# The channel part of a Fourier block: jobs in a written order across steps, no GpSimd, and a plain first step for the second batch

## The chip, the cores and the metric

The kernel runs on one core of a Trainium2 chip. The metric is device time in microseconds of one execution; the kernel before takes 647.47 us (median of three runs, 646.49 to 647.83). The engines are named as in the trace: PE is TensorE's matmul, PEld its weight load, DVE is VectorE, ACT is ScalarE, POOL is GpSimd, SP is SyncE, whose queue issues most DMAs.

## The reference

Two batches of 768 tokens go through three blocks: bucketed attention, a gated convolution block and a Fourier block. The change lies in the last one:

```
X = fft(fft(x, axis=1), axis=2)
u = x + real(X)
un = (u - mean(u)) / sqrt(var(u) + 1e-6)
ch = max(un @ w_ch1, 0) @ w_ch2        # w_ch1: 512 x 2048, w_ch2: 2048 x 512
out = u + ch
```

The last two lines with the normalisation are called the channel part here. The weights come as float64.

## The kernel before, in words

Matmuls run on float32 values split in two parts, a high part of few mantissa bits and a low part that holds the rest, so that each product is three matmuls: high by high, high by low and low by high. Any operand of a matmul therefore needs an ACT copy that rounds to the high part and a DVE subtraction that gives the low part.

*Mixing.* The function `mixing` computes the Fourier transform of both batches. Its loop has 14 turns. From turn 8 on it also prepares batch 0 for the channel part: `stats` (mean and variance on DVE, then a square root on ACT), `scale` (reciprocal and shift on DVE, then two ACT activations that write the normalised `un`), `u_transpose` on PE and `u_parts` (high part `bh` on ACT, low part `bl` on DVE). Tiles of tokens are treated in pairs `kt` and `kt + 3`, so there are three such pairs per batch. Behind the loop the last transform of batch 1 is added up (`both`), and POOL writes `u[1]`.

*Channel part.* The hidden width of 2048 is cut in 16 blocks `f` of 128. A block's first layer (`first`) is 12 matmuls per half of the tokens (128 by 384), its relu is taken as high part on ACT and low part on DVE (`relu_high`, `relu_low`), and its second layer (`second(m, t)`) is three matmuls (128 by 512) for each of six token tiles `t`, which add up in six PSUM banks `acc`. When the batch changes, the six sums are added into `u` on DVE.

Batch 0 does blocks 0 to 3 in this plain way (`PLAIN`). Everything else goes in 14 steps of one batch and two blocks each, where the four products of a 2 by 2 block matrix are made with seven products of half size (a Strassen scheme; `product`, six matmuls each). It needs sums of weights (`weight_steps`, four jobs: two sums, four combinations, high part, low part) and sums of tokens (`token_steps`, the same four; for batch 1 `turned`, which also transposes). Seven products share two PSUM tiles `x` and `y`; their interim results are copied to `snap` by ACT (lines 1651, 1662, 1665), added to by DVE (1654, 1671, 1674), and then go through the relu.

Weights are loaded as float64 chunks of 512 KB (`channel_load`) and turned into high and low part by integer arithmetic, six jobs a chunk (`channel_steps`, lines 148 to 171: six DVE instructions, two on ACT). A step converts two chunks.

Each engine runs its instructions in the order in which the program issues them. That order is set by hand: a step calls its products one after the other, and between them `after(c)` runs the background jobs (conversion of weights, weight sums, token sums) that a small table has put at place `c`, always those of the same step. Some of the sums run on POOL (`eng=nc.gpsimd`): the low parts of batch 1's token sums, the weight sums for blocks 0 to 3 and 6, 7, and two thirds of batch 0's token sums.

Of the kernel before, what the change touches and what calls it, by code (L numbers as in the profile page):

```python
# [37 lines left out]
PLAIN = 4  # L38

# [67 lines left out]
def block_kernel(  # L107
# [24 lines left out]
    def from64(words_of, raw, dst, half=False, parts=P, spare=False):  # L132
# [7 lines left out]
        a, e, g = (words_of(n, x)[:parts] for x in "aeg")  # L140
# [6 lines left out]
        def s0():  # L147
            nc.vector.tensor_scalar(a, hi, 0x7FFFFE00, None, op0=ALU.bitwise_and)

        def s1():  # L150
            nc.scalar.activation(a, a, AF.Relu, scale=8.0, bias=col[:parts, b : b + 1])

        def s2():
            nc.vector.tensor_scalar(g, hi, 0x1FF, 15, op0=ALU.bitwise_and, op1=ALU.logical_shift_left)
            nc.vector.scalar_tensor_tensor(g, lo, 17, g, op0=ALU.logical_shift_right, op1=ALU.bitwise_or)

        def s3():
            nc.vector.scalar_tensor_tensor(a, hi, -(2 ** 31), a, op0=ALU.bitwise_and, op1=ALU.bitwise_or)  # L158
            nc.vector.tensor_scalar(e, a, -(2 ** 23), None, op0=ALU.bitwise_and)

        def s4():
            if spare:
# [7 lines left out]
        def s5():  # L170
            nc.scalar.copy(dst()[0], fold(a.bitcast(F32)))  # L171
# [834 lines left out]
    def channel_steps(k, spare=False):  # L1006
# [5 lines left out]
        st = from64(channel_words, wraw[k], lambda: w, spare=spare)  # L1012
        third = st[3]

        def last_words():
            third()
            channel_load(k + 2)

        st[3] = last_words
        return st  # L1020

    def stats(b, kt):

        for t in (kt, kt + 3):
            st = wst[0].tile([P, 6], F32, tag="st", name="st")
            nc.vector.bn_stats(st, u[b][:, t, :])
            nc.vector.bn_aggr(mu[b][:, t, :], st)
        ks = slice(kt, kt + 4, 3)
        nc.scalar.activation(rstd[0][:, b, ks], mu[b][:, ks, 1], AF.Sqrt, bias=col[:, 6:7])

    def scale(b, kt):
# [3 lines left out]
        nc.vector.scalar_tensor_tensor(m, mu[b][:, ks, 0], -1.0, r, op0=ALU.mult, op1=ALU.mult)  # L1035
        for t in (kt, kt + 3):
# [17 lines left out]
    def mixing(es):  # L1054
# [248 lines left out]
        for i in range(len(jobs) + 2):  # L1303
# [63 lines left out]
    def channel(es):  # L1367
# [19 lines left out]
        sh, sl = {}, {}  # L1387

# [3 lines left out]
        def plain_b(b, j, k):  # L1392
            if b == 1 and k == 1:
                return [k1[:, x, :].rearrange("p (c t) -> p c t", c=2) for x in range(2)]
# [36 lines left out]
        def weight_steps(n, eng=nc.vector):  # L1431
# [9 lines left out]
            def add():  # L1441
                combos(eng, box["x"], "w")
                sh[n], sl[n] = (fp.tile([P, 4, 2, P], F32R, tag=f"s{y}", name="s", bufs=2) for y in "hl")

            def high():
                split(box["x"], sh[n], sl[n], eng)[0]()

            def low():
                split(box["x"], sh[n], sl[n], eng)[1]()
# [29 lines left out]
        def turned(r):  # L1479


            x = temp()
            for k in range(2):
                pu = u_transpose(1, 3 * k + r, tile_f)
                nc.scalar.copy(x[:, 2 * k : 2 * k + 2].rearrange("p a c t -> p (a c t)"), pu)
            ts_ = slice(r * P, (r + 1) * P)
            k1h, k1l = plain_b(1, 1, 1)
            src = x[:, 0:2].rearrange("p a c t -> p (a c) t")
            hi = bh[1, 0][:, :, ts_]
            nc.scalar.copy(hi, src)  # L1490
            nc.scalar.copy(k1h[:, :, ts_], x[:, 3])
            nc.vector.tensor_tensor(bl[1, 0][:, :, ts_], src, f32(hi), op=ALU.subtract)
            nc.vector.tensor_tensor(k1l[:, :, ts_], x[:, 3], f32(k1h)[:, :, ts_], op=ALU.subtract)
            return token_steps(1, r, x, low_eng=nc.gpsimd)[1:]
# [14 lines left out]
        def first(f, k):  # L1509
            w1h, w1l = w1[f % 5]  # L1510
            pf = (tile_a(2 + k) if f == 1 else tile_f())[:, :HS]
            n = 0
            for w, x in ((w1h, bh[0, k]), (w1l, bh[0, k]), (w1h, bl[0, k])):
                for c in range(NC):
                    nc.tensor.matmul(pf, w[:, c, :], x[:, c, :], start=n == 0, stop=n == 3 * NC - 1)
                    n += 1
            relu_high(pf, f, k)
            relu_low(pf, f, k)
# [33 lines left out]

        def second(m, t):
            b, f = units[m]
            begin = m == 0 or units[m - 1][0] != b
            end = m == len(units) - 1 or units[m + 1][0] != b
# [5 lines left out]
            for n, (x, w) in enumerate(((hh, w2h), (hh, w2l), (hl, w2h))):  # L1562
                nc.tensor.matmul(accs[t], x[:, ts_], w, start=begin and n == 0, stop=end and n == 2)  # L1563
            if end:
                if all(x[0] != b for x in units[m + 1 :]):
                    result(b, t)
                else:
                    nc.vector.tensor_tensor(u[b][:, t, :], accs[t], u[b][:, t, :], op=ALU.add)


        run(wnext)

        stats(1, 0)
        waiting = []
        for f in range(PLAIN):
            for k in range(2):
                first(f, k)
            if f == 0:
                scale(1, 0)
                stats(1, 1)  # L1580
                continue
            if f == 1:
                scale(1, 1)
                stats(1, 2)
                ws_ = weight_steps(0, nc.gpsimd)
            cs_ = channel_steps(4 + f)
            for t in range(6):
                second(f - 1, t)
                if t in (0, 3) and f == 1 or t == 1 and f == 2:
                    waiting.append(turned((t // 3 if f == 1 else 2)))  # L1590
                if t in (1, 4) and f == 1 or t == 3 and f == 2:
                    run(waiting[-1][:1])
                if t in (2, 5) and f == 1 or t == 4 and f == 2:
                    run(waiting[-1][1:])
                if t == 1 and f == 1:
                    scale(1, 2)
                if t == 5 and f == 1:
                    run(ws_[:2])
                if t == 5 and f == 2:
                    run(ws_[2:])  # L1600
                run(cs_[t : t + 1])


        for i, (b, n) in enumerate(steps):
            m = PLAIN + 2 * i
            fa, fb = 2 * n, 2 * n + 1
            k = 8 + 2 * i
            ca, cb = channel_steps(k), channel_steps(k + 1)
            bg = {}

            def at(c, *fs):
                bg.setdefault(c, []).extend(fs)

            at(0, ca[0], ca[2])
            at(1, ca[1])
            at(2, *ca[3:])
            if i % 2:
                at(5, cb[0], cb[2])
                at(7, cb[1])
                at(9, cb[3])  # L1620
                at(10, *cb[4:])
            else:
                at(3, cb[0], cb[2])
                at(4, cb[1])
                at(5, *cb[3:])
            if i in (0, 3):
                wt = weight_steps({0: 1, 3: 3}[i], nc.gpsimd)
                for c, x in zip((0, 1, 8, 8), wt):
                    at(c, x)
# [101 lines left out]
```

## Time and profile before

| | before |
|---|---|
| median of three runs | 647.47 us |
| the profiled execution: time | 650.17 us |
| the profiled execution: span on the core | 648.2 us |
| mean granted PE clock over the span | 0.984 of full speed |
| PE busy | 604.5 us (93%) |
| DVE busy | 543.5 us (84%) |
| ACT busy | 377.1 us (58%) |
| POOL busy | 286.6 us (44%) |

The span runs from the first to the last instruction on the core; the time of the profiled execution holds some 2 us more. The channel part begins with the first plain product at 352.41 us and its last matmul ends at 644.4 us; what lies behind is the last addition and the output DMA. Busy times count an instruction's latency, so instructions that overlap in an engine's pipeline count once where they overlap. An idle time is put down to the engine whose result came last.

### The profile page before, as it was taken

How to read it: one execution, taken by the hardware profiler on the slowest of the kernel's cores; microseconds unless marked ns; L12 is line 12 of the kernel's file. 1: busy time of each engine (PE TensorE's matmuls, PEld its weight loads, DVE VectorE, ACT ScalarE, POOL GpSimd, SP SyncE). 2: the span in 40 equal slices, each digit the busy share in tenths (PEclk: the TensorE clock that was granted, in tenths of full speed). 3: DMA queues.
4: the chain of work that ended last, by engine and by line, in shares of the span. 5: the costliest groups of instructions: out<-in, count | busy, mean ns of one | idle time of the engine just before them, and what ended most of it. 6: DMA issues, size and time to landing. Idle time of an engine off the chain costs nothing.

```text
span 648.2 us, 10436 instructions
## 1 busy us (share of the span) xinstructions
PE 604.5 (93%) x3627; PEld 546.9 (84%) x3627; DVE 543.5 (84%) x1012; ACT 377.1 (58%) x748; POOL 286.6 (44%) x336
## 2 busy tenths in 40 slices
PE   8999999999999999999989697897899999999997
PEld 7889999999888899988969585676688898888896
DVE  5999999999898997997888668888888888888635
ACT  5989989899888888636264633333243434343320
POOL 7243588777789897943404178434420000000000
PEclk9999999999999999999999888997999999999999
DMA  6956577675846611430111012113021212121004
GB/s 138 213 127 162 153 155 174 153 181 134 191 122 175 163 43 40 175 144 7 59 55 44 0 33 65 66 33 99 0 66 65 70 62 70 61 75 56 2 32 163
DMA packets 54958, 62.03 MB, mean 96 GB/s; under 512 B 29184, under 2 KB 42664, under 8 KB 54650
## 3 DMA queue, kind: packets, MB, share of 16 engines
q1 hardware_dynamic: 54170, 57.81, 33.8%
q0 software_dynamic: 432, 3.55, 1.4%
q8 instruction: 29, 0.48, 0.3%
q14 instruction: 23, 0.19, 0.1%
q10 hardware_dynamic: 304, 0.01, 0.0%
HBM read 36.74 MB, written 3.19 MB: 62 GB/s over the span
## 4 chain that ended last, share of the span: by engine, by line
PE 45%; DVE 29%; ACT 7%; DMA 6%; issue 5%; POOL 5%; SPq 2%; POOLq 0%; ACTq 0%; DVEq 0%
PE acc L1563 10%; PE pf L1524 9%; PE sp L560 5%; PE op L619 4%; PE ptp L596 3%; DMA qk<-ht 3%; DVE ptl L608 3%; DMA xs<-xc 3%; PE ps L224 3%; DVE sd L571 3%; PE ps L1203 3%; DVE cv L158 2%; DVE hid L1507 2%; PE ps L1267 2%; ACT hid L1503 1%
## 5 line engine op out<-in xcount | busy, mean ns | idle before, releaser
L571 DVE TENSOR_SCALAR_CACHE_REDUCE sd<-sp 128x768 f32<-128x768 f32 x96 | 91.1, 950 | 8.3 <-PE sp L560 7.7
L608 DVE TENSOR_TENSOR ptl<-ptp,pth 128x768 fp32r<-128x768 f32 x96 | 91.5, 953 | 6.4 <-ACT pth L604 3.8
L560 PE MATMUL sp<-qk 128*128 128x512 f32 (+1 forms) x384 | 91.4, 359 | 4.9 <-DVE sd L571 2.7
L578 ACT ACTIVATE sd<-sd,nm 128x768 f32<-128x768 f32 x96 | 90.2, 939 | 1.5 <-DVE sd L571 1.5
L604 ACT CAST pth<-ptp 128x768 fp32r<-128x768 f32 x96 | 77.1, 804 | 18.3 <-PE ptp L696 9.2
L596 PE MATMUL ptp<-ident,sd 128*128 128x128 f32 x576 | 78.5, 272 | 0.2 <-ACT sd L578 0.2
L619 PE MATMUL op<-pth,v 128*128 128x256 f32 x288 | 74.0, 283 | 2.1 <-ACT xc L632 2.1
L619 PE MATMUL op<-ptl,v 128*128 128x256 f32 x288 | 73.8, 286 | 0.0
L1563 PE MATMUL acc<-vh,hid 128*128 128x512 f32 x192 | 66.8, 404 | 4.5 <-ACT vh L171 4.2
L560 PEld LDWEIGHTS sp<-qk 128*128 128x128 f32 x384 | 58.2, 189 | 14.9 <-DVE sd L571 7.8
L596 PEld LDWEIGHTS ptp<-ident,sd 128*128 128x128 f32 x576 | 65.8, 140 | 1.1 <-ACT sd L578 0.5
L1524 PE MATMUL pf<-t,s 128*128 128x384 f32 x252 | 52.0, 348 | 13.1 <-ACT snap L1662 6.0
L1524 PEld LDWEIGHTS pf<-t,s 128*128 128x128 f32 x252 | 45.4, 194 | 19.8 <-ACT snap L1662 8.6
L1503 ACT ACTIVATE hid<-snap 128x384 fp32r<-128x384 f32 x42 | 21.4, 522 | 69.5 <-DVE snap L1674 40.4
L637 POOL TENSOR_TENSOR xm<-xc,xs 64x256 f32<-64x256 f32 x48 | 35.3, 736 | 59.1 <-DMA xs<-xc 38.3
L619 PEld LDWEIGHTS op<-pth,v 128*128 128x128 f32 x288 | 54.2, 188 | 7.1 <-ACT xc L632 3.2
L619 PEld LDWEIGHTS op<-ptl,v 128*128 128x128 f32 x288 | 54.2, 188 | 0.2
L1563 PEld LDWEIGHTS acc<-vh,hid 128*128 128x128 f32 x192 | 37.2, 194 | 12.6 <-ACT vh L171 4.6
L243 POOL TENSOR_TENSOR g<-g,conv_tmp 128x768 f32<-128x768 f32 x27 | 46.7, 1729 | 1.2
L1507 DVE SCALAR_TENSOR_TENSOR hid<-snap,hid 128x384 fp32r<-128x384 f32 x42 | 23.7, 573 | 18.0 <-ACT hid L1503 18.0
L1563 PE MATMUL acc<-vl,hid 128*128 128x512 f32 x96 | 38.7, 403 | 0.0
L1563 PE MATMUL acc<-gl,hid 128*128 128x512 f32 x144 | 37.1, 394 | 0.0
(313 smaller groups left out, 1415.8 us busy)
## 6 DMA issues: line engine op xcount, KB each, us to landing
raw<-in_moe_w_ch_dram SPq DMA_DIRECT2D x32, 512.0 KB
qk<-ht SPq DMA_DIRECT2D x60, 192.0 KB
qk<-lt SPq DMA_DIRECT2D x30, 192.0 KB
rqk<-in_q_dram SPq DMA_DIRECT2D x16, 192.0 KB
rqk<-in_k_dram SPq DMA_DIRECT2D x16, 192.0 KB
rv<-in_v_dram SPq DMA_DIRECT2D x8, 384.0 KB
out_dram<-o SPq DMA_DIRECT2D x12, 256.0 KB
xs<-xc SPq DMA_DIRECT2D x47, 64.0 KB
```

Of the source, the lines that this page charges most:

```text
L243: nc.gpsimd.tensor_tensor(dst, dst, tmp, op=ALU.add)
L560: nc.tensor.matmul(sp[:, cs], q2[i][:, m, qi * P : (qi + 1) * P], k2[i][:, m, cs], start=m == order[0], stop=m == order[1])
L571: nc.vector.tensor_scalar(sd[n], sp, CLAMP, None, op0=ALU.min, op1=ALU.min, accum_out=st[p]["nm"][:, n % 12 : n % 12 + 1],)
L578: nc.scalar.activation(sd[n], sd[n], AF.Exp, bias=st[p]["nm"][:, i : i + 1], scale=-1.0, accum_out=st[p]["sums"][:, i : i + 1],)
L596: nc.tensor.transpose(tp[:, r // 3, c0 : c0 + P], sd[n][:, r * P : (r + 1) * P], ident)
L604: nc.scalar.copy(p_parts(n)[0], tp)
L608: nc.vector.tensor_tensor(lo, tp, f32(ho), op=ALU.subtract)
L619: nc.tensor.matmul(po[kb], v3[:, r, c0 : c0 + P], pt[kb][x][:, r, :], start=r == 0 and x == 0, stop=r == R - 1 and x == 1,)
L637: add[kb] = lambda: nc.gpsimd.tensor_tensor(st[p]["xm"][mr, blk * QB : (blk + 1) * QB], xc[mr, :], xs[mr, :], op=ALU.add)
L1507: nc.vector.scalar_tensor_tensor(hl, src, 0.0, f32(hh), op0=ALU.max, op1=ALU.subtract)
L1524: nc.tensor.matmul(to, a[x][:, c, :], b_[y][:, c, :], start=not more and n == 0, stop=n == 5, skip_group_check=more,)
L1563: nc.tensor.matmul(accs[t], x[:, ts_], w, start=begin and n == 0, stop=end and n == 2)
```

## The change

The background jobs and the products of all steps become named jobs, and a table `ORDERS` of 16 strings (one for the plain part, 14 steps, the tail) says in which order they are issued. A name with a minus is a job of the step before, with a plus one of the step after. Names: `I` plain product, `M1` to `M7` the seven products, `F` and `G` second layer of the block before and of this step's first block, `s`, `c` copies to and additions into `snap`, `h`, `l` the relu's high and low part, `A`, `B` the two chunks of weights with their jobs 0 to 6 (job 6 is the load of the chunk after next), `W` weight sums, `T`, `U` token sums, `f` the additions into `u` (now a job apart from `second`).

No job uses POOL any more: all sums run on DVE. The first step of batch 1 (blocks 0 and 1) is done with eight plain products (four of 12 matmuls), so the weight sums for it fall away, and there are two more tiles for token parts (`sums`, `spare_r`). In `mixing`, `stats` and `scale` are cut in three parts, and the parts come one turn later. The rest of the kernel is as before.

```diff
@@ two of the 16 strings: the steps 1 (batch 1) and 2 (batch 1)
+M1 B5- B6- B4- M2 W0 s0 F0 c11 F1 W1 h11 M6 l11 M5 W2 A0 T0 F2 s1 s3 F3 A1 W3 M7 A3 M3 A5 c22 F4 c12 F5 A2 h12
+M4 h22 l12 A6 l22 G0 h21 T1 G1 G2 l21 T2 G3 A4 G4 T0+ G5
+M1 T3- M2 s0 U0 F0 c11 F1 B0- h11 M6 T1 B1- M5 s1 l11 T2 U1 F2 s3 F3 M7 B3- U2 M3 B2- B5- c22 F4 B6- c12 F5
+B4- h12 M4 h22 U3 G0 h21 l12 G1 l21 G2 T3 G3 l22 G4 A0 G5 A2 A1
@@ def stats(b, kt)
             nc.vector.bn_aggr(mu[b][:, t, :], st)
+
+    def root(b, kt):
         ks = slice(kt, kt + 4, 3)
         nc.scalar.activation(rstd[0][:, b, ks], mu[b][:, ks, 1], AF.Sqrt, bias=col[:, 6:7])
@@ def scale(b, kt)
         nc.vector.scalar_tensor_tensor(m, mu[b][:, ks, 0], -1.0, r, op0=ALU.mult, op1=ALU.mult)
+
+    def normal(b, kt):
         for t in (kt, kt + 3):
@@ def mixing(es), the loop's turns from 8 on
                 else:
-                    scale(0, i - 9)
+                    root(0, i - 9)
+                if i == 10:
+                    scale(0, 0)
+                    normal(0, 0)
                 stats(0, i - 8)
...
             elif i > 10:
+                if i == 11:
+                    root(0, 2)
                 for t in (i - 11, i - 8):
                     u_parts(t, u_transpose(0, t, psum))
-                if i == 11:
-                    scale(0, 2)
+                if i < 13:
+                    scale(0, i - 10)
+                    normal(0, i - 10)
                 run(wnext.pop(0) for _ in wnext[:1])
@@ def channel(es)
+        sums = fp.tile([P, 12, 2, P], F32, tag="t0l", name="sums")
+        spare_r = fp.tile([P, 4, HS], F32R, tag="snap", name="bq")
...
-            return token_steps(1, r, x, low_eng=nc.gpsimd)[1:]
+            more = token_steps(1, r, x, low_eng=nc.vector)
...
+        def follow(i, order):
+            for x in order.split():
+                n = x.strip("+-")
+                jobs[i + x.count("+") - x.count("-")][n]()
...
+            if i == 0:
+                for f in (fa, fb):
+                    jobs.update(plain_jobs(b, f))
+            else:
+                jobs.update(product_jobs())
+            for z, k in (("A", 8 + 2 * i), ("B", 9 + 2 * i)):
+                if k < 2 * NF:
+                    for q, job in enumerate(channel_steps(k, load=False)):
+                        jobs[f"{z}{q}"] = job
+            made = {0: (1, nc.vector), 1: (2, nc.vector), 3: (3, nc.vector)}.get(i)
...
+        jobs += [step_jobs(i) for i in range(len(steps) + 1)]
+        for i, order in enumerate(ORDERS):
+            follow(i, order)
```

Two places show how instructions move. The first is ACT's queue at the end of the mixing loop. `un` is the normalised batch 0 (one row is one pair of tiles), `bh` its high part behind the transposes, `a` and `ft` belong to the transform of batch 1, `gl` is a weight chunk, and the `a` in the last row of the second piece is what the first matmuls of the last transform read. Before:

```order
L1213 COPY y<-ps 128x512
L1037 ACTIVATE un<-u_4303,shift,rstd 128x512 x2
L1029 ACTIVATE rstd<-mu_4305,col 128x2
L1243 CAST a<-ps 128x258
L1228 CAST ft<-pw 128x256
L1213 COPY y<-ps 128x512
L1051 CAST bh_4310<-ps 128x4x128
L1051 CAST bh_4312<-ps 128x4x128
L1037 ACTIVATE un<-u_4303,shift,rstd 128x512 x2
L1248 ACTIVATE a<-ps,y 128x258
L1228 CAST ft<-pw 128x256
```

And now, from the same place on:

```order
L1296 COPY y<-ps 128x512
L1110 ACTIVATE rstd<-mu_4305,col 128x2
L1134 CAST bh_4310<-ps 128x4x128
L1134 CAST bh_4312<-ps 128x4x128
L1120 ACTIVATE un<-u_4303,shift,rstd 128x512 x2
L1331 ACTIVATE a<-ps,y 128x258
L1311 CAST ft<-pw 128x256
L1134 CAST bh_4310<-ps 128x4x128
L1134 CAST bh_4312<-ps 128x4x128
L1120 ACTIVATE un<-u_4303,shift,rstd 128x512 x2
L249 CAST gl<-cv 128x512
L1326 CAST a<-ps 128x258
```

The last `un` row of the piece before is the third pair; in the changed kernel the second pair stands there, and the third follows behind the next two `bh` rows and in front of the last `gl` and `a`.

The second is DVE's queue at the first addition into `snap` of step 2 (blocks 4 and 5 of batch 1), which the product `M5` waits for. `t` are token sums of batch 0, `x` the sums before they are split, `cv` the integer words of a weight chunk, `hid` the relu. Before:

```order
L1427 TENSOR_TENSOR s<-x,s 128x1024
L1507 SCALAR_TENSOR_TENSOR hid<-pf,hid 128x384
L158 SCALAR_TENSOR_TENSOR cv<-raw,cv 128x512
L159 TENSOR_SCALAR cv<-cv 128x512
L166 SCALAR_TENSOR_TENSOR gl<-cv 128x512
L1427 TENSOR_TENSOR t_5595<-x,t_5594 128x8x128
L148 TENSOR_SCALAR cv<-raw 128x512
L154 TENSOR_SCALAR cv<-raw 128x512
L155 SCALAR_TENSOR_TENSOR cv<-raw,cv 128x512
L1654 TENSOR_TENSOR snap<-snap,pf 128x384
L1507 SCALAR_TENSOR_TENSOR hid<-snap,hid 128x384
```

And now:

```order
L1494 TENSOR_TENSOR x<-bh_4310,bl_4311 128x512
L1494 TENSOR_TENSOR x<-bh_4312,bl_4313 128x512
L1521 TENSOR_TENSOR t_5548<-x,t_5547 128x8x128
L1494 TENSOR_TENSOR x<-bh_4310,bl_4311 128x512
L1494 TENSOR_TENSOR x<-bh_4312,bl_4313 128x512
L1750 TENSOR_TENSOR snap<-snap,pf 128x384
L221 TENSOR_SCALAR cv<-raw 128x512
L1506 TENSOR_TENSOR x<-x 128x256
L1507 TENSOR_TENSOR x<-x 128x256
L1508 TENSOR_TENSOR x<-x 128x256
L1509 TENSOR_TENSOR x<-x 128x256
L1617 SCALAR_TENSOR_TENSOR hid<-snap,hid 128x384
```

Before, seven background instructions stood between the last relu and the addition, and the relu's low part followed it at once. Now the token sums that ran on POOL stand there, the conversion comes behind the addition, and five instructions stand between the addition and the relu's low part.

## Rows read from the trace of the kernel before

**Rows 1.** Busy us (instructions) per stretch: PE, PEld, DVE, ACT, POOL; clock, DMA, GB/s.
```profile
352.40:505.00 152.60, 128.23 (x609) 111.26 (x608) 125.08 (x210) 59.76 (x107) 62.47 (x68) 0.94 0.15 47
505.00:644.40 139.40, 137.37 (x679) 122.03 (x677) 102.53 (x192) 46.77 (x88) 0.00 (x0) 1.00 0.18 61
644.40:648.20 3.80, 0.02 (x1) 0.00 (x0) 0.75 (x2) 0.00 (x0) 0.00 (x0) 1.00 0.62 238
```
**Rows 2.** Waits of PE in the channel part: total us, times, longest.
```profile
PE pf L1524 <- ACT snap L1662: 6.0, 6, 1.6
PE pf L1515 <- ACT x L1485: 5.5, 1, 5.5
PE pf L1524 <- DVE snap L1654: 5.4, 3, 3.7
PE acc L1563 <- ACT vh L171: 4.2, 1, 4.2
```
**Rows 3.** Timeline, PE, where it runs without a wait: start us, us.
```profile
614.55 1.55 PE L1563 MATMUL acc<-gl,hid 128*128 128x512 f32 x6
615.94 1.21 PE L1524 MATMUL pf<-t,s 128*128 128x384 f32 x6
616.98 0.85 PE L1524 MATMUL pf<-bh,s 128*128 128x384 f32 x4
```
**Rows 4.** Timeline, DVE, where it runs back to back and POOL is idle.
```profile
508.40 1.28 DVE L1568 TENSOR_TENSOR u<-acc,u 128x512 f32<-128x512 f32 x2
509.60 0.55 DVE L1507 SCALAR_TENSOR_TENSOR hid<-snap,hid 128x384 fp32r<-128x384 f32 x1
510.06 0.55 DVE L1507 SCALAR_TENSOR_TENSOR hid<-pf,hid 128x384 fp32r<-128x384 f32 x1
...
516.58 0.69 DVE L158 SCALAR_TENSOR_TENSOR cv<-raw,cv 128x512 int32<-128x512 int32 x1
...
519.78 0.69 DVE L158 SCALAR_TENSOR_TENSOR cv<-raw,cv 128x512 int32<-128x512 int32 x1
```
**Rows 5.** Timeline, DVE, a weight sum that ran on DVE.
```profile
428.88 0.68 DVE L1400 TENSOR_TENSOR x<-wh,wl 128x512 f32<-128x512 f32 x1
...
430.19 0.43 DVE L1407 TENSOR_TENSOR x<-x 128x256 f32<-128x256 f32 x1
430.65 0.42 DVE L1408 TENSOR_TENSOR x<-x 128x256 f32<-128x256 f32 x1
...
435.51 1.22 DVE L1427 TENSOR_TENSOR s<-x,s 128x1024 fp32r<-128x1024 f32 x1
```
**Rows 6.** DVE 352 to 490 by form: busy us, mean ns; idle before, releaser.
```profile
L155 DVE SCALAR_TENSOR_TENSOR cv<-raw,cv 128x512 int32<-128x512 int32 x13 | 11.1, 852 | 0.4
L1507 DVE SCALAR_TENSOR_TENSOR hid<-snap,hid 128x384 fp32r<-128x384 f32 x13 | 8.0, 613 | 6.7 <-ACT hid L1503 6.7
...
L1026 DVE BATCH_NORM_STATS2 st<-u 128x6 f32<-128x512 f32 x6 | 4.0, 673 | 0.0
```
**Rows 7.** Timeline of all engines, end of the mixing loop.
```profile
340.49 1.52 ACT L1037 ACTIVATE un<-u,shift,rstd 128x512 f32<-128x512 f32 x2 [2.27 <-DVE shift L1035]
...
343.48 0.64 ACT L171 CAST gl<-cv 128x512 fp32r<-128x512 f32 x1
343.63 1.03 PE L1044 MATMUL ps<-ident,un 128*128 128x128 f32 x8
344.00 0.40 ACT L1243 CAST a<-ps 128x258 fp32r<-128x258 f32 x1
344.27 1.11 ACT L1051 CAST bh<-ps 128x512 fp32r<-128x512 f32 x2
344.42 1.31 PE L1267 MATMUL ps<-a,seq 128*128 128x258 f32 x9
344.92 1.29 DVE L1052 TENSOR_TENSOR bl<-ps,bh 128x512 fp32r<-128x512 f32 x2
```
**Rows 8.** Timeline, PE, the product M5 of step 2.
```profile
445.23 2.29 PE L1524 MATMUL pf<-t,s 128*128 128x384 f32 x6 [3.73 <-DVE snap L1654]
```

More of the change, by code (lines that the diff above doesn't have):

```diff
@@ L139, in from64, with word @@
         lo, hi = words[:, :, 0], words[:, :, 1]
-        a, e, g = (words_of(n, x)[:parts] for x in "aeg")
+        got = {}
+        def word(x):
+            if x not in got:
+                got[x] = words_of(n, x)[:parts]
+            return got[x]
         b = 4 if half else 3
@@ L1011, in channel_steps, with step @@
         w = w2[f % 4] if i else w1[f % 5]
[L1012 to L1020, printed above, removed]
+        st = []
+        def step(q):
+            if not st:
+                st.extend(from64(channel_words, wraw[k], lambda: w, spare=spare))
+            st[q]()
+            if q == 3 and load:
+                channel_load(k + 2)
+        return [lambda q=q: step(q) for q in range(6)] + [lambda: channel_load(k + 2)] * (not load)
     def stats(b, kt):
@@ L1442, in add, with parts @@
                 combos(eng, box["x"], "w")
-                sh[n], sl[n] = (fp.tile([P, 4, 2, P], F32R, tag=f"s{y}", name="s", bufs=2) for y in "hl")
+            def parts():
+                return fp.tile([P, 4, 2, P], F32R, tag="sh" if n not in sh else "sl", name="s", bufs=2)
             def high():
-                split(box["x"], sh[n], sl[n], eng)[0]()
+                sh[n] = parts()
+                split(box["x"], sh[n], None, eng)[0]()
             def low():
+                sl[n] = parts()
                 split(box["x"], sh[n], sl[n], eng)[1]()
@@ new lines, in second, with flush @@
+                nc.tensor.matmul(accs[t], x[:, ts_], w, start=begin and n == 0, stop=ends(m) and n == 2)
+        def flush(m, t):
+            b = units[m][0]
+            if all(x[0] != b for x in units[m + 1 :]):
+                result(b, t)
+            else:
+                nc.vector.tensor_tensor(u[b][:, t, :], accs[t], u[b][:, t, :], op=ALU.add)
+        def follow(i, order):
+            for x in order.split():
+                n = x.strip("+-")
+                jobs[i + x.count("+") - x.count("-")][n]()
@@ new lines, in channel, with plain_jobs @@
+        jobs, pfs = [{}], {}
+        def plain_jobs(b, f):
+            out = {}
+            for k in range(2):
+                n = f"{f}{'ab'[k]}"
+                out["I" + n] = lambda k=k: pfs.__setitem__((b, f, k), first(f, k, b))
+                out["h" + n] = lambda k=k: relu_high(pfs[b, f, k], f, k)
+                out["l" + n] = lambda k=k: relu_low(pfs[b, f, k], f, k)
+            return out
+        for f in range(PLAIN):
+            jobs[0].update(plain_jobs(0, f))
+            for t in range(6):
+                jobs[0][f"S{f}{t}"] = lambda f=f, t=t: second(f, t)
@@ L1685, in channel, with pf @@
[L1685 to L1692 removed]
+            S2, S4, S3, S1 = (lambda j=j: [w[n][:, j] for w in (sh, sl)] for j in range(4))
+            T1, T4, T3, T2 = (lambda j=j: [w[:, j] for w in tq[b]] for j in range(4))
+            tiles = {}
+            def pf(x):
+                if x not in tiles:
+                    tiles[x] = tile_f()[:, :HS]
+                return tiles[x]
```

288 lines of the change are left out of this document (153 added, 135 removed).

## The prediction

> **What bounds the kernel now.** I read the stretches first, then PE's waits, then what stands behind them. The channel part lasts from 352.4 to 644.4, 292.0 us, and splits at 505 [rows 1]. Behind 505 PE is busy 137.4 of 139.4 us at full clock: it is the bound there. Ahead of 505 it is busy 128.2 of 152.6 us at a mean clock of 0.94, while DVE is busy 125.1 and POOL 62.5 us. What PE would need alone follows from a stretch without waits [rows 3]: six second-layer matmuls start 1.39 us before the next group (614.55 to 615.94), six of a product 1.04 us (615.94 to 616.98). The part has 96 groups of the first kind, 114 of the second (16 plain, 98 in products) and 24 transposes at 1.03 us per eight [rows 7]: 133.4 + 118.6 + 3.1 = 255.1 us. So 36.9 us are lost. Per matmul that is 0.198 us; the 609 matmuls ahead of 505 need 120.6 us and lose 32, the 679 behind it 134.4 us and lose 5 [rows 1]. The loss to be won sits in the first half.
>
> The four longest groups of PE's waits make 21.1 us [rows 2]. By name they are mostly ACT's (copies to `snap` and of a transposed tile, the high part of a weight chunk), but each of these ACT instructions follows DVE or POOL. One shows it plainly: M5 of step 2 waits 3.73 us [rows 8] for an addition that, in DVE's queue, stands behind three instructions of a chunk which nobody needs yet (the second pair of order pieces). DVE itself is not full there. It waits 6.7 us for ACT because the relu's low part follows its high part at once, and its conversions take 852 ns in the mean [rows 6], against 0.69 us for an instruction of the same kind with POOL idle [rows 4]. The first half is bound by DVE's queue: by its order, its waits and its slowed instructions.
>
> **The change part by part.** *PE.* The plain first step has eight products for seven, one group more: +1.0 us, 256.1 us in all. This is the least that the channel part can take.
>
> *DVE.* Everything that POOL did comes to DVE, and the order is fixed. I count DVE's work in the first twelve strings (plain part and steps 0 to 10), since all conversions and sums lie there, at start-to-start distances. A chunk takes 3.20 us (516.58 to 519.78, six instructions [rows 4]); 27 chunks and one last job of 0.6 make 87.0. 52 relu low parts at 0.46 (509.60 to 510.06) make 23.9; 30 additions into `snap`, of the same shape, 13.8; 30 additions into `u` at 0.60 (two from 508.40 to 509.60) 18.0 [rows 4]. Ten four-job sums take 1.31 + 4 x 0.46 + 1.22 = 4.37 each [rows 5], 43.7. Three transposed tiles take a split (1.6, an estimate: one such sum of 512 columns and two of 256), four combinations (1.84) and a low part (1.22) [rows 5], 13.9. Statistics are 4.0 [rows 6] and, with their small ones, some 6. Sum: 206.3 us. These are prices without POOL beside it; that the slowing goes is the gain from leaving POOL out, and it about pays for the work that comes over.
>
> In the same twelve strings PE has 94 x 1.04 + 75 x 1.39 + 3.1 = 205.1 us, and behind them 21 x 1.04 + 21 x 1.39 = 51.0 us against DVE's 39 instructions or 20.5 us. So both engines have the same work for 205 us, in lock step, and then PE alone. A step of the table is some 15.5 us of either. Since jobs that are not urgent stand in DVE's queue ahead of urgent ones, a loss on DVE can't be made up later within these strings: the queue as a whole, not only its urgent part, must keep up.
>
> How well does an engine do that is bound in its own order? PE shows 137.4 of 139.4, 0.985; DVE in the first half shows 125.1 of 152.6, 0.82, in an order with the waits named above [rows 1]. The new order puts other work between high and low part of a relu and takes the addition forward, so most of these waits have cover: the work that hides ACT's half microsecond is the next DVE job in the string. If that cover is too short, DVE stands still as before. I take 0.96, near to PE's value, since both pieces of order that I compared have cover: 206.3 / 0.96 = 214.9 us. DVE also starts late: the low part of the second product needs two products (4.2 us) and a relu (some 0.6), and until then DVE has had some 2.4 us of work: 2.4 us behind.
>
> *Mixing.* Normalising comes one turn later, and this costs. The slot at 340.49, in which ACT normalised the third pair, now holds the second [rows 7]. Its transposes end at some 342.6; then come two copies (1.11) and behind the first of them two subtractions (1.29), which end at 344.6; reciprocal and shift 0.3; normalising 1.52, until 346.4; in front of the last transform's first operand still a copy of a chunk and its own (343.48 to 344.40, 0.92). The transform starts at 347.4 instead of 344.42: +3.0 us, with PE idle. Nothing else can go in front of it, as the queue is in order. Bounds: 0, if the chain is shorter than its rows, and 4. I take 3.0; the channel part starts at 355.4.
>
> *At nothing.* Loads are a job of their own now and stand a few jobs later. DMA moved 61 GB/s at a share of 0.18 [rows 1], so some 340 GB/s when busy: 512 KB take 1.5 us, and over half a step of some 15 us lies between a load and its first use. Tiles taken later, or more of them, add no instruction.
>
> *Sum.* 355.4 + 2.4 + 214.9 + 51.0 + 3.8 (tail [rows 1]) = 627.5 us of span against 648.2. The execution's time is 2.0 us over its span, and the median of the runs 2.7 us under that execution, so the median is 0.7 under the span: 626.8, say 627 us.
>
> **Rivals.** *PE alone is the bound.* If DVE's order leaves no gap, the span is 355.4 + 256.1 + 3.8 = 615.3, a median of 614.6. For it: the sums are equal, and PE has shown 0.985. Against it: two engines that wait for each other in turn lose more than one that waits for none; at 0.985 of DVE the median is already 621.3. Without the loss in mixing it would be 611.6.
>
> *DVE saturated, slower than before.* The twelve strings keep DVE busy with all 206.3 us, and PE has some two microseconds of work between an addition's product and the next product on the same PSUM tile. If each step has a few waits for ACT or PE which the next job doesn't cover, they add up over twelve strings, PE stands still with DVE, and its pauses lower the clock as ahead of 505. The point of decision: the span reaches 648.2 when the strings take 648.2 - 355.4 - 2.4 - 51.0 - 3.8 = 235.6 us, a share of 0.876. At the 0.82 of the first half before it would be 251.6, a median of 663.5. For it: 0.82 is what DVE has shown here, with POOL taking part of the work. Against it: that share was reached with the waits of [rows 6], one of which alone (6.7 us) is 4% of the stretch. The Trainium skill speaks for this rival (Perfetto Trace Analysis, Optimizing Scalar/DVE Operations): where DVE is saturated, some of its work may go to ScalarE or even GpSimd; this change does the reverse. The same place adds that the two share a read port, so that shifting work between them may not help; the 852 ns against 0.69 us agree with that.
>
> *The order helps, but half of it is lost again.* At a share of 0.88 to 0.90 the median would be 641 to 646: faster, outside my forecast.
>
> **How the numbers follow.** Forecast (share 0.90 to 0.99, medians 620 to 641): 0.76. PE alone, 614 to 620: 0.12. Half lost, 641 to 646: 0.02. Within 0.2% (1.3 us, about what a measurement of this kernel can tell from no change): 0.02. Slower: 0.08. So faster 0.90, same 0.02, slower 0.08. The range takes in PE's bound and reaches to the share of 0.90: 615 to 641.
>
> **What would show it.** Right: POOL empty behind some 360; DVE's L155 of before (L230 now) at 0.69 us in the mean throughout; DVE busy over nine tenths until some 570 and PE over nine tenths with it; no wait of PE over 2 us behind 380; the clock at full speed where it was 0.94; the first plain product some 3 us later than 352.4, with a gap of PE in front of the last transform. Wrong: PE waits for DVE in every step at the same place (then the sharing of DVE is the bound, and its share tells the time), DVE's instructions as slow as before with POOL idle (then POOL was not what slowed them), or a plain product at 352.4 (then the chain in mixing was hidden). A time over 641 means that the order left waits uncovered.

## The result and the profile after

The changed kernel takes 612.2 us (median of four runs, 610.8 to 613.5); the kernel before took 647.65 us in its four runs beside it. The ratio is 0.9451, with a 95% interval of 0.942 to 0.9483: 35.5 us faster. The forecast was 627 us with a range of 615 to 641. The direction was right; the kernel is faster than the range allowed, and comes out at the rival "PE alone is the bound", in its form without the loss in mixing (611.6).

The stretches of the profile after, cut where its channel part begins (351.95), at 505 as before, and behind its last matmul; the columns are those of [rows 1]:

```profile
351.95:505.00 153.05, 152.99 (x783) 138.41 (x782) 149.17 (x294) 74.31 (x132) 4.76 (x4) 1.00 0.20 63
505.00:607.90 102.90, 102.90 (x511) 92.01 (x509) 72.29 (x135) 33.35 (x63) 0.00 (x0) 1.00 0.17 58
607.90:611.70 3.80, 0.10 (x1) 0.00 (x0) 0.83 (x2) 0.00 (x0) 0.00 (x0) 0.89 0.65 246
```

PE is busy in 255.9 of 256.0 us, at full clock throughout; ahead of 505 it was 128.2 of 152.6 us at 0.94 [rows 1]. It gets through 783 matmuls ahead of 505 instead of 609. The channel part lasts 256.06 us (351.95 to 608.01) instead of 292.01. Of these 36 us, 26.4 are the idle time of PE before (152.60 - 128.23 and 139.40 - 137.37 [rows 1]). The other 9.6 are matmuls that took longer: PE was busy for 265.6 us before and 256.0 now, with one product's work more, and its granted clock ahead of 505 was 0.94 and is 1.00.

The view of waits, PE, from the end of the mixing to the end of the kernel (total us, times, longest) holds two groups:

```profile
PE ps L1127 <- ACT un L1120: 3.0, 2, 1.8
PE ps L1321 <- DVE ft L1312: 1.2, 1, 1.2
```

Both lie in the mixing. All groups of [rows 2] are gone, and with them M5's 3.73 us [rows 8]: behind 351.95 there is no wait of PE at all. DVE's waits in the twelve strings (352 to 556) have shrunk to three:

```profile
DVE cv L234 <- ACT cv L225: 0.3, 1, 0.3
DVE hid L1617 <- ACT hid L1613: 0.2, 1, 0.2
DVE snap L1750 <- PE pf L1635: 0.2, 1, 0.2
```

Before, ahead of 505 alone, its two largest waits were for the relu's high part and for the high part of batch 1's transposed tokens:

```profile
DVE hid L1507 <- ACT hid L1503: 12.4, 17, 1.4
DVE bq L1492 <- ACT bq L1490: 7.7, 3, 3.6
```

The forms that answer to [rows 6], DVE, 352 to 490 (busy us, mean ns, idle before):

```profile
L230 DVE SCALAR_TENSOR_TENSOR cv<-raw,cv 128x512 int32<-128x512 int32 x17 | 11.8, 692 | 0.6
L1617 DVE SCALAR_TENSOR_TENSOR hid<-snap,hid 128x384 fp32r<-128x384 f32 x16 | 8.7, 552 | 0.0
```

The conversion takes 692 ns instead of 852, the relu's low part 552 instead of 613, with no idle time in front of it instead of 6.7 us. The first and last rows of DVE's work in the twelve strings, and what follows it there:

```profile
352.83 0.68 DVE L1105 BATCH_NORM_STATS2 st<-u 128x6 f32<-128x512 f32 x1
...
555.59 0.69 DVE L243 SCALAR_TENSOR_TENSOR vl<-cv 128x512 fp32r<-128x512 int32 x1
559.32 0.56 DVE L1750 TENSOR_TENSOR snap<-snap,pf 128x384 f32<-128x384 f32 x1 [3.04 <-PE pf L1635]
```

From 352.83 to 556.28 are 203.4 us without a gap worth the name, against PE's 205.05 us for the same strings (351.95 to 557.0, busy in 204.99). Only behind them does DVE wait for PE (3.04 us).

The end of the mixing, where [rows 7] stood:

```profile
336.57 1.52 ACT L1120 ACTIVATE un<-u,shift,rstd 128x512 f32<-128x512 f32 x2 [2.25 <-DVE shift L1116]
...
340.91 1.52 ACT L1120 ACTIVATE un<-u,shift,rstd 128x512 f32<-128x512 f32 x2 [1.03 <-DVE shift L1116]
...
341.78 1.97 PE L1127 MATMUL ps<-ident,un 128*128 128x128 f32 x8 [1.23 <-ACT un L1120]
342.33 0.60 ACT L249 CAST gl<-cv 128x512 fp32r<-128x512 f32 x1
342.84 0.36 ACT L1326 CAST a<-ps 128x258 fp32r<-128x258 f32 x1
343.11 1.26 ACT L1134 CAST bh<-ps 128x512 fp32r<-128x512 f32 x2
343.40 1.87 PE L1350 MATMUL ps<-a,seq 128*128 128x258 f32 x9
```

The order is the one predicted: second pair, third pair, `gl`, `a`, the transform. But the last transform starts at 343.40, 1.0 us earlier than before and not 3.0 later.

The medians agree with this: of the 36 us that the channel part lost, 35.5 arrive in the median, so all that lies ahead of it costs about 0.5 us by this and not 3.0 (the interval of the ratio is some 2 us wide on either side, and the 36 us are read from one execution of each kernel).

### The profile page after: what moved, and what is told of

It reads as the page before. It is cut to its first block, busy times and chain, and to the rows that moved or that the text cites. A ratio compares the mean times of both kernels' runs of the same rounds, so it can differ in the third digit from the quotient of the medians.

```text
span 611.7 us, 10422 instructions
## 1 busy us (share of the span) xinstructions
PE 595.0 (97%) x3633; PEld 544.6 (89%) x3633; DVE 537.4 (88%) x1041; ACT 378.3 (62%) x747; POOL 228.9 (37%) x272
## 4 chain that ended last, share of the span: by engine, by line
PE 68%; DVE 18%; DMA 4%; ACT 3%; issue 2%; SPq 2%; POOL 2%; POOLq 0%; DVEq 0%; ACTq 0%
PE acc L1676 20%; PE pf L1635 14%; PE sp L638 6%; PE op L697 6%; PE ptp L674 5%; DVE sd L649 4%; DVE ptl L686 4%; PE pf L1625 3%; PE ps L302 3%; PE ps L1286 3%; DMA qk<-ht 3%; PE ps L1350 2%; PE late L302 1%; DMA xs<-xc 1%; PE early L302 1%
## 5 line engine op out<-in xcount | busy, mean ns | idle before, releaser
L1676 PE MATMUL acc<-vh,hid 128*128 128x512 f32 x192 | 64.0, 391 | 0.0
L1635 PE MATMUL pf<-t,s 128*128 128x384 f32 x234 | 45.1, 335 | 0.0
L1635 PEld LDWEIGHTS pf<-t,s 128*128 128x128 f32 x234 | 41.3, 188 | 2.7 <-DVE snap L1750 0.3
L1613 ACT ACTIVATE hid<-snap 128x384 fp32r<-128x384 f32 x39 | 19.6, 521 | 33.3 <-DVE snap L1750 30.2
L1750 DVE TENSOR_TENSOR snap<-snap,pf 128x384 f32<-128x384 f32 x39 | 21.1, 549 | 20.0 <-PE pf L1635 19.9
L225 ACT ACTIVATE cv<-cv,col 128x512 int32<-128x512 int32 x32 | 23.1, 722 | 24.6 <-DVE cv L221 24.4
## 6 DMA issues: line engine op xcount, KB each, us to landing
out_dram<-o SPq DMA_DIRECT2D x12, 256.0 KB
```

The costliest lines, as they stand in the source:

```text
L1635: nc.tensor.matmul(to, a[x][:, c, :], b_[y][:, c, :], start=not more and n == 0, stop=n == 5, skip_group_check=more,)
```

## Experiments

Each kernel was timed beside the kernel before. "Channel part" is the time from the first plain product to the last matmul in a kernel's own profile, and so free of what the stages ahead of it took (its start lies between 348.5 and 355.3 us in these profiles, for kernels with the same code up to there too). It is read from one execution of each kernel. The changed kernel has 256.06.

| kernel | median us | ratio to before (95%) | channel part us |
|---|---|---|---|
| changed kernel | 612.2 | 0.9451 (0.942 to 0.9483) | 256.06 |
| e1, old order in the steps 1 to 13 | 632.56 | 0.9745 (0.9703 to 0.9788) | 274.44 |
| e9, old order in the plain part and step 0 | 623.72 | 0.9632 (0.9606 to 0.9659) | 267.33 |
| e2, before without GpSimd | 647.27 | 0.999 (0.9959 to 1.0021) | 290.44 |
| e3, changed, GpSimd given its sums back | 615.93 | 0.9493 (0.9443 to 0.9543) | 258.57 |
| e4, changed, relu's low part right behind the high | 618.74 | 0.9547 (0.9502 to 0.9591) | 261.29 |
| e12, 6 us more on DVE | 618.49 | 0.954 (0.9503 to 0.9578) | 260.99 |
| e5, 12 us more on DVE | 626.8 | 0.9673 (0.9649 to 0.9697) | 268.15 |
| e6, 24 us more on DVE | 641.07 | 0.9892 (0.9866 to 0.9918) | 281.67 |
| e7, 17 us less on DVE | 609.91 | 0.9409 (0.9375 to 0.9444) | 255.45 |
| e10, seven products in the first step of batch 1 | 622.36 | 0.9612 (0.9581 to 0.9642) | 264.97 |
| e8, normalising as before | 613.16 | 0.9451 (0.9426 to 0.9475) | 256.03 |
| e11, third pair behind a sum | 609.46 | 0.9408 (0.9385 to 0.9431) | 255.84 |

### Which part of the change made it faster

**e1** puts the strings of the steps 1 to 13 (and those jobs of the tail that belong to them) in the order of the kernel before, without GpSimd and with the plain part as changed. One string of 14:

```diff
-M1 T3- M2 s0 U0 F0 c11 F1 B0- h11 M6 T1 B1- M5 s1 l11 T2 U1 F2 s3 F3 M7 B3- U2 M3 B2- B5- c22 F4 B6- c12 F5
-B4- h12 M4 h22 U3 G0 h21 l12 G1 l21 G2 T3 G3 l22 G4 A0 G5 A2 A1
+M1 s0 A0 A2 T0 M2 c11 h11 l11 A1 F0 F1 A3 A6 A4 A5 T1 M6 s1 B0 B2 M5 s3 B1 F2 F3 B3 B6 B4 B5 M7 c22 M3 c12 h12 l12
+F4 F5 h22 l22 T2 T3 M4 h21 l21 U0 G0 G1 U1 G2 G3 U2 G4 G5 U3
```

> The changed kernel (no GpSimd, plain first step, mixing as changed) with steps 1 to 13 in the order of places of the kernel before; only the plain part and step 0 keep the written order. Theory 'order' (PE lost its 32 us to jobs in the wrong places of DVE's queue): at least half of the gain is lost, 630 us or more, with PE waits of 1 to 4 us for the first addition into snap again. Rival 'GpSimd' (DVE was slowed by GpSimd beside it): order does not matter, below 618 us.

The channel part is 18.4 us longer than that of the changed kernel, half of what was won. PE's waits in it are again mostly for the copy to `snap` and the addition into it, as in [rows 2] (channel part, total us, times, longest):

```profile
PE pf L1623 <- DVE snap L1738: 7.1, 4, 2.6
PE pf L1623 <- ACT snap L1735: 4.0, 5, 1.4
PE acc L1664 <- ACT hid L1601: 0.7, 1, 0.7
PE pf L1623 <- DVE hid L1605: 0.6, 1, 0.6
```

**e9** is the other half: the plain part and step 0 in the old order, everything behind it as changed.

```diff
-c45 I0a I0b st0 h0a l0a sq0 I1a rs0 h0b st1 no0 l0b I1b sq1 h1a c44 rs1 l1a no1 st2 tr0 ur0 tc0 S00 c50 h1b
...
+c44 c45 st0 sq0 I0a h0a l0a I0b h0b l0b rs0 no0 st1 sq1 I1a h1a l1a I1b h1b l1b rs1 no1 st2 sq2
...
```

> The plain part and step 0 issue their jobs in the order of the kernel before (without GpSimd, with the plain part's sums on VectorE), every later step and the second batch in the written order. Theory (lock step: TensorE and VectorE have nearly the same work in the channel part, so what TensorE waits for at the front can't be made up later): the front is two of the fourteen steps, but it is where before had most of its long waits; the loss is 15 to 17 us, channel part 270 to 274 us, median 626 to 630. Rival (VectorE works ahead later and gives the loss back): channel part under 262 us, median under 619.

It costs 11.3 us of the channel part (11.5 of the median). The stretches, cut at 400, show that all of it is lost at the front and none is made up behind it:

```profile
351.56:400.00 48.44, 40.14 (x207) 35.80 (x206) 35.36 (x78) 23.37 (x44) 5.21 (x4) 0.93 0.11 33
400.00:618.90 218.90, 218.86 (x1087) 195.72 (x1085) 185.62 (x351) 83.84 (x150) 0.00 (x0) 1.00 0.19 64
```

PE idles 8.3 us ahead of 400, 5.8 of them in one wait for a transposed tile (`sums`), and hardly any behind it, where it is the bound. The size I expected (15 to 17 us) was too large, but the rival that the loss would be recovered is out. The two halves of the order add up to 18.4 + 11.3 = 29.7 of the 36 us. No run of the changed kernel has both in the old order at once, and the other 6 us are not taken apart; GpSimd (e2, e3) and the plain first step (e10) are among them.

**e2** takes GpSimd alone out of the kernel before (`nc.gpsimd` becomes `nc.vector` in the four places), nothing else.

> The kernel before with every sum of the channel part on DVE instead of GpSimd, each in its old place; nothing else changed. Theory 'order': the 20 us of sums that come over and the slowing that goes cancel, 640 to 655 us. Rival 'GpSimd': the slowing was the loss, below 630 us.

No difference can be measured. DVE's instructions become as fast as in the changed kernel (e2, DVE's first 138 us of the channel part; the same row of before, 852 ns, is in [rows 6]):

```profile
L155 DVE SCALAR_TENSOR_TENSOR cv<-raw,cv 128x512 int32<-128x512 int32 x13 | 9.0, 693 | 0.4
```

But DVE has the sums as well (busy 131.27 of 156.51 us up to 505), and PE's waits are those of before, 6.7 us on the copy to `snap` and 5.1 on the addition. What DVE gets back in speed about pays for the work that comes over, and with this order neither shows in the time.

**e3** gives GpSimd its sums back in the changed kernel (the same four kinds of jobs, the strings unchanged).

> The changed kernel, written order kept, with the sums that GpSimd did before given back to it (low parts of batch 1's token sums, weight sums of two steps, token sums of two tiles of batch 0). Theory 'order': GpSimd is no loss by itself, within 4 us of 612. Rival 'GpSimd': its sums take nearly twice DVE's time and slow DVE's conversions from 0.69 to 0.85 us, 622 us or more.

2.5 us of channel part (3.7 of the median, the intervals overlap). PE waits 1.4 us in all. DVE is rid of these sums, but its busy time in the channel part falls by 1.9 us only (221.6 to 219.7), because its other instructions slow down beside GpSimd (last section). In this order, then, GpSimd's absence is worth some 2.5 us, a fourteenth of the gain.

**e4** puts each relu's low part right behind its high part, as in the kernel before (in step 2, `h11 M6 T1 B1- M5 s1 l11` becomes `h11 l11 M6 T1 B1- M5 s1`), which takes the cover away.

> The changed kernel with every low part of a relu issued right behind its high part, all else in the written order. If cover between the two is what keeps DVE's queue going, DVE waits about half a microsecond up to 52 times in the first twelve strings, and as DVE and PE have equal work there, the time rises by 10 to 25 us (622 to 637). If DVE runs so far ahead of PE that waits don't matter, it stays within 3 us of 612.

5.2 us of channel part, 6.5 of the median: less than the 10 to 25 us that I expected and more than the rival's 3, so DVE has some lead, but not enough to do without the cover. The relu's spacing is a sixth of what the order brings. The rest must lie in the places of the other jobs, of which no run moves one kind alone.

### Is DVE full, and how much room is there?

**e5, e6, e12** repeat an instruction of the conversion that does nothing new, once per chunk, twice per chunk, and once in every second chunk.

```diff
             nc.vector.tensor_scalar(g, hi, 0x1FF, 15, op0=ALU.bitwise_and, op1=ALU.logical_shift_left)
+            nc.vector.tensor_scalar(g, hi, 0x1FF, 15, op0=ALU.bitwise_and, op1=ALU.logical_shift_left)
```

> The changed kernel with one more DVE instruction per weight chunk of the channel part and of the mixing end (the first instruction of the second conversion job is issued twice; the result is the same): 27 x 0.45 = 12 us more work for DVE in the first twelve strings, 6%. If DVE had no room (the prediction's lock step, DVE's share 0.96 as a loss for PE): 8 to 12 us more, 620 us or more. If DVE ran ahead of PE by enough: within 3 us of 613.

> As before with two more DVE instructions per chunk, 24 us more work for DVE, 12%. DVE then has some 228 us in strings in which PE has 205: any theory has DVE as the bound; 613 + 24 less the room there was. Without room 635 or more; with a room of 4% 625 to 630.

> The changed kernel with every second chunk of the weight conversion given one VectorE instruction more that does nothing new (the same shift again): about 13 instructions of 0.45 us, 6 us, spread evenly over the channel part; 12 us of the same cost 12.1 us there. Theory (VectorE's queue is full and ends together with TensorE's, so that there is hardly room): 4 to 6 us slower, median 616 to 618.5, ratio 0.951 to 0.955. Rival (a few us of room in the buffers between the two engines, and the 12 us cost that much for another reason, such as a tile that comes free late): under 2 us, median under 614.5.

27 x 0.45 = 12.2 us lengthen the channel part by 12.1 us, 24.3 by 25.6, and 14 x 0.45 = 6.3 by 4.9. The smallest dose leaves 1.4 us uncharged, close to the difference between PE's 205.05 us and DVE's 203.4. This room is read from one profile; by the medians (6.3 us for 6.3, with intervals of 2 us and more) there may be none, and the larger doses leave 0.1 and -1.3 us, with pauses of PE that cost more than themselves (last section). The waits of e5 lie where the prediction's lock step has them (PE, total us, times, longest):

```profile
PE pf L1636 <- DVE snap L1751: 5.2, 7, 1.8
PE pf L1636 <- ACT snap L1748: 0.9, 2, 0.4
PE pf L1128 <- DVE hid L1618: 0.4, 1, 0.4
```

These are 6.5 of the 12.1 us; part of the rest are matmuls that run slower behind a wait (last section). The median of e5 is 14.6 us longer, as its channel part also begins later (354.44).

**e7** leaves out the second instruction of that job, some 17 us of DVE's work; the low parts of the channel weights lack their lowest bits in it.

```diff
-            nc.vector.scalar_tensor_tensor(g, lo, 17, g, op0=ALU.logical_shift_right, op1=ALU.bitwise_or)
```

> The changed kernel without the second instruction of the second conversion job of each chunk (the low words are left out, so the low parts of the channel weights are not right): 27 x 0.65 = 17 us less work for DVE. If PE alone bounds the channel part: no change, within 2 us of the changed kernel. If DVE still costs PE time in any step: 3 us or more less.

The channel part shortens by 0.6 us. The median is 2.3 us shorter, between the two answers that I had laid down, but the profile has most of that ahead of the channel part (it begins at 348.80). In the part itself DVE's relief buys nearly nothing:

```profile
348.80:604.25 255.45, 255.44 (x1292) 230.57 (x1290) 207.40 (x401) 108.17 (x194) 4.75 (x4) 1.00 0.19 61
```

PE is busy in 255.44 of 255.45 us. The changed kernel stands where both limits meet.

**e10** gives the first step of batch 1 its seven products back: one product's work less for PE in that step, the weight sums for blocks 0 and 1 more on DVE (the four jobs `X` in the strings of the plain part). Shown is one line of that string; the string of the step itself is replaced by one for seven products.

```diff
-bl2 W2+ I3b h3a c73 c75 c76 l3a c74 S20 h3b ta0 S21 S22 l3b th0 S23 ta1 S24 S25 ta2 th1
+bl2 W2+ X0 X1 I3b h3a c73 c75 c76 l3a c74 S20 h3b ta0 S21 S22 l3b X2 th0 S23 X3 ta1 S24 S25 ta2 th1
```

> Batch 1's first step has seven products again, with the weight sums of the other batch's blocks on VectorE before it, the rest as in the changed kernel. TensorE loses one product's work per chunk there, VectorE gains four additions, together about 4.5 us by the weight-sum rows. Theory (VectorE is at the edge, a microsecond added to it is one added to the time): 3 to 4.5 us slower, median 615.5 to 617, ratio about 0.952. Rival (TensorE's count alone sets the time): about 1 us faster, median 611, ratio 0.9435.

8.9 us of channel part, twice what I expected. The direction speaks for the theory, the size doesn't come from DVE's work alone. Around that step:

```profile
380.00:396.00 16.00, 11.09 (x43) 8.61 (x42) 15.09 (x26) 6.36 (x9) 0.00 (x0) 0.79 0.11 33
```
```profile
386.49 0.40 PE L1672 MATMUL acc<-vh,hid 128*128 128x512 f32 x1
390.19 1.65 PE L1631 MATMUL pf<-t,s 128*128 128x384 f32 x4 [3.31 <-ACT snap L1746]
393.28 2.07 PE L1631 MATMUL pf<-t,s 128*128 128x384 f32 x4 [1.44 <-DVE t L1517]
```
```profile
385.18 0.41 DVE L1502 TENSOR_TENSOR sums<-sums 128x256 f32<-128x256 f32 x1
...
388.60 1.22 DVE L1517 TENSOR_TENSOR s<-x,s 128x1024 fp32r<-128x1024 f32 x1
389.74 3.49 DVE L1517 TENSOR_TENSOR t<-sums,t 128x1024 fp32r<-128x1024 f32 x3
```

The seven products want the combined token sums `t` of batch 1 at the step's start; the plain products don't read them. In e10 DVE works through them back to back (15.09 of 16 us), ACT's copy to `snap` comes in its queue only behind the casts of `t` at 389.67, and PE waits 4.75 us. From the first of these waits on the matmuls are slow as well: the granted clock is 1.00 up to 389, 0.50 from 389.5 to 399 and 1.00 again from 399.5, and PE's busy time in the channel part is 259.7 us for less work than the 256.0 of the changed kernel. The string was not made for that, so e10 shows what this insertion costs, not what the best order of seven products would.

### The mixing

**e8** has the normalising of the kernel before in the changed kernel.

```diff
-                    root(0, i - 9)
-                if i == 10:
-                    scale(0, 0)
-                    normal(0, 0)
+                    scale(0, i - 9)
+                    normal(0, i - 9)
+                root(0, i - 8)
...
                 if i == 11:
+                    scale(0, 2)
+                    normal(0, 2)
```

> The changed kernel with the normalising of batch 0 in the turns of the kernel before. By the prediction's chain (the third pair's normalising ends 3.0 us later): 3 us less than the changed kernel, 0.9405 of the kernel before. By the two traces, laid side by side from the end of the attention on (the first plain product 1.3 us later): 1.3 us less, 0.943. If the old place costs PE as much by ACT's wait for the variance: no change, 0.945.

No difference: 613.16 against 612.2, the same ratio, which rules out the 3 us but not 1.3. Measured from a group of matmuls that all these kernels share (PE, the last `ps<-tab,ft` x12, at 324.55 before, 322.77 after, 322.34 here), the first plain product comes 27.9 us later before, 29.2 after and 29.4 here. In e8, then, the 1.3 us between before and after are there with the old normalising too. But one profile can't settle so little: in e1, e3, e4, e9 and e10, whose code up to there is that of the changed kernel, the same stretch takes 28.3 to 30.3 us, and in e2, with the code of before, 27.9. Whether the new places cost about a microsecond stays open.

**e11** issues the third pair's normalising later, behind the loop, and its transposes behind the first sum of the last transform, so that PE has the transform's work where it waited 1.23 us.

```diff
-                for t in (i - 11, i - 8):
-                    u_parts(t, u_transpose(0, t, psum))
                 if i < 13:
+                    for t in (i - 11, i - 8):
+                        u_parts(t, u_transpose(0, t, psum))
                     scale(0, i - 10)
-                    normal(0, i - 10)
+                if i == 11:
+                    normal(0, 1)
...
+        normal(0, 2)
         run(wnext.pop(0) for _ in range(3))
         both(1, 0)
+        for t in (2, 5):
+            u_parts(t, u_transpose(0, t, psum))
```

> Only the end of the mixing changes: the third pair's normalising and transposes are issued behind the first of the last transform's sums, so that TensorE finds work where it waited 1.2 us for ScalarE. Theory (the wait and the lower clock after it go): 1 to 2 us faster than the changed kernel, ratio about 0.943. Rival (the wait is moved behind the sum, since the plain part needs the same parts): no change, 0.945.

609.46 us, the fastest kernel with the full result. Its interval (0.9385 to 0.9431) just touches that of the changed kernel. In the profile the gap is gone:

```profile
338.48 1.66 PE L1321 MATMUL ps<-tab,ft 128*128 128x258 f32 x6
339.93 1.95 PE L1350 MATMUL ps<-a,seq 128*128 128x258 f32 x9
...
343.76 1.04 PE L1127 MATMUL ps<-ident,un 128*128 128x128 f32 x8
...
349.45 1.55 PE L1629 MATMUL pf<-bh,w 128*128 128x384 f32 x8
```

From the shared group (322.47 here) the plain product comes after 27.0 us instead of 29.2, and less than the 28.3 to 30.3 of all kernels with the changed kernel's mixing. 1.2 us of the 2.2 are the wait; the rest goes with the granted clock, which is 0.72 from 338 to 344 here and 0.50 in the changed kernel.

## Why the prediction was wrong

The bound was read rightly as the order and the waits of DVE's queue (e1, e9); its slowed instructions, named beside them, were worth little by themselves (e2, e3). Right were also the floor of 256.1 us (measured 256.06), the equal work of both engines in the twelve strings, the empty POOL, L230 at 0.69 us, the full clock and the missing waits. One of the signs of being wrong came as well: a plain product at 352, where the chain in mixing was to move it by 3 us. The span came out at 611.7, 15.8 us under the forecast's 627.5. It splits like this:

| term | predicted us | measured us | difference |
|---|---|---|---|
| start of the channel part | 355.4 | 351.95 | -3.45 |
| DVE's late start and its twelve strings | 2.4 + 214.9 | 205.05 (PE's) | -12.25 |
| PE behind them | 51.0 | 51.0 | 0 |
| tail | 3.8 | 3.7 | -0.1 |

**The step that failed is "206.3 / 0.96 = 214.9 us".** The 206.3 us themselves were 1.4% too high (203.4 measured). The division cost 8.6 us, and it was wrong in kind. The prices were distances from start to start, so the gaps between instructions were already in them: a queue with no wait at all takes just their sum. The 0.985 and 0.82 that I set beside it were shares of busy time, a different measure; in the changed kernel DVE is busy in 198.19 of the 203.37 us from 352.83 to 556.20, a share of 0.975, while it hardly waits (0.7 us in all). What could lengthen the sum was waits alone; the prediction argued that most of them had cover and named none without it. On that reading the sum had to stand undivided, within 1.2 us of PE's 205.1. e4 and e12 show that the worry itself was real: without the cover the part is 5.2 us longer, and there is room for no more than a microsecond or two.

**The late start of 2.4 us** was added to a chain that it isn't on. DVE begins its strings 0.9 us behind PE (352.83 against 351.95) and ends 0.7 ahead (556.28 against 557.0), so its start takes up half of the 1.6 us that its queue is shorter, and no more. When two engines end together, a delay of one counts only as far as it exceeds the other's remainder.

**Mixing's 3.0 us** decided about the range. Its lower end, 615, was PE's bound with a channel part that starts at 355.4; with this term at nothing that bound is 611.6, and the measured 612.2 lies just above. The term was too large, because I held the slot in ACT's queue fixed at 340.49. It moves: `un` of the first pair, 1.52 us, stands one turn later too, and the wait of 2.17 us that a `rstd` at 327.44 had is gone. Counted from the shared group of matmuls, the second `un` row of [rows 7] lies at 15.9 us before, and the same slot at 13.8 after. The chain behind it is as long as I worked out; it starts 2.1 us earlier, and 0.8 us are left of it for the transform's start. By e8 and the medians the change costs less than 3 us there; whether it costs these 0.8, the runs can't tell. That the start is even earlier than before (351.95 against 352.41) is what the stages ahead took in that execution, since the shared group begins 1.8 us sooner in it (322.77 against 324.55): the -3.45 us of the table hold that much luck.

**The rivals.** "PE alone" was the truth. It had a chance of 0.12 for 614 to 620 us; its form without the loss in mixing, 611.6, was written down, but no chance was given to any time under 614. The case against it (two engines that wait for each other lose more than one) fell with the profile after: DVE's queue, 1.6 us shorter than PE's, never made PE wait. "DVE saturated, slower" named the right danger: 12 us more work cost all of 12 us (e5). The Trainium skill (Perfetto Trace Analysis, Optimizing Scalar/DVE Operations) holds out GpSimd for a saturated DVE, with the warning on the shared port; here the warning is borne out, since the channel part is 2.5 us longer when GpSimd takes work from the full DVE (e3). e1, e2 and e9 show where the gain comes from: the order in the steps (18.4 us), the order at the front (11.3), and without a new order nothing from GpSimd (0.999).

## What to carry to other kernels

Price an in-order queue from start to start and add only the waits that you can name; don't divide such a sum by a share of busy time. Where two engines have the same work over a long stretch, as here, start from the longer of the two sums; what decides is whether each wait has another job behind it to fill it, which the order of the queue tells. Before you charge a chain that is moved in a queue, move everything ahead of it in that queue as well. And give the range the room of every term: here its lower end kept one of them at full size.

## What the runs showed of the hardware

*GpSimd slows only some of DVE's instructions.* e3 against the changed kernel, DVE from 352 to 490, the same instructions with GpSimd at work (first fence, e3) and without (second):

```profile
L230 DVE SCALAR_TENSOR_TENSOR cv<-raw,cv 128x512 int32<-128x512 int32 x17 | 13.5, 792 | 0.6
L1617 DVE SCALAR_TENSOR_TENSOR hid<-snap,hid 128x384 fp32r<-128x384 f32 x16 | 10.3, 652 | 0.3 <-ACT hid L1613 0.3
L229 DVE TENSOR_SCALAR cv<-raw 128x512 int32<-128x512 int32 x17 | 8.6, 503 | 0.1
L1617 DVE SCALAR_TENSOR_TENSOR hid<-pf,hid 128x384 fp32r<-128x384 f32 x15 | 8.0, 546 | 2.0 <-ACT hid L1613 2.0
```
```profile
L1617 DVE SCALAR_TENSOR_TENSOR hid<-pf,hid 128x384 fp32r<-128x384 f32 x15 | 8.1, 549 | 0.2 <-ACT hid L1613 0.2
L229 DVE TENSOR_SCALAR cv<-raw 128x512 int32<-128x512 int32 x17 | 7.2, 423 | 0.1
```

With two inputs from SBUF, 692 becomes 792 ns and 552 becomes 652; with one of them from PSUM (`pf`), 549 stays 546. These are means over a stretch in which GpSimd is at work for only some 49 of 138 us, so an instruction that meets it loses more than the 100 ns. The Trainium skill (SBUF — State Buffer, Who interferes with whom) says that an instruction with two SBUF inputs contends with GpSimd's reads, and the rows agree. The shift with a single SBUF input slows as well, from 423 to 503 ns.

*A wait of PE can cost more than itself.* In e5, six matmuls of a product behind the longest wait, and those of the next two products (PE, start us, us):

```profile
476.19 1.33 PE L1636 MATMUL pf<-t,s 128*128 128x384 f32 x6 [1.84 <-DVE snap L1751]
...
479.88 1.64 PE L1636 MATMUL pf<-t,s 128*128 128x384 f32 x6
481.35 1.20 PE L1636 MATMUL pf<-bq,s 128*128 128x384 f32 x6
```

The granted clock is 1.00 up to 477, 0.50 (the lower of its two levels, 1.2 GHz) from 477.5 to 480.5 and 1.00 again from 481; PE had stood still for 1.84 us before it fell. In the stretches of 10 us with waits of 0.5 to 1.0 us it stayed at 1.00. Why e5 costs more than its waits (12.1 us against 6.5) is open beyond that.
